# When lists are scattered and rows gathered: spacing the indirect transfers at the seam between attention and the experts

## The chip, the core and the metric

The kernel runs on one core of one Trainium2 chip. A core has five engines with queues of their own: PE (TensorE, matrix products), DVE (VectorE), ACT (ScalarE), POOL (GpSimd) and SP (SyncE, which here only issues transfers). Each engine executes its instructions strictly in the order in which they stand in its queue, and waits at an instruction until the semaphores it names have been reached. Transfers between the chip's main memory and the core's buffers are carried out by 16 DMA engines, which all queues share. Ordinary transfers are issued by SP; indirect ones, whose rows are picked by a list of indices, are issued by POOL.

The metric is the device time of one execution in microseconds (us): 654.73 us before the change, the median of three runs. One more execution was recorded by the profiler; all views of the trace come from it.

## The reference, cut to what matters

```python
# attention: B, H, S, D = 4, 8, 768, 48
f = 1.0 / (1.0 + np.exp(-f_logit))
for t in range(S):
    state = f[:, :, t, :, None] * state + np.einsum('bhd,bhe->bhde', k[:, :, t], v[:, :, t])
    y[:, :, t] = np.einsum('bhd,bhde->bhe', q[:, :, t], state)
x = y.transpose(0, 2, 1, 3).reshape(3072, 384)
# experts: E = 8, F = 1024
noisy = x @ w_gate + np.log1p(np.exp(x @ w_noise)) * noise
top2 = np.argpartition(-noisy, 2, axis=1)[:, :2]
# weights of the two: softmax over their noisy logits
for e in range(8):
    for k in range(2):
        mask = top2[:, k] == e
        h = np.maximum(x[mask] @ w1[e], 0.0)
        out[mask] += top2_w[mask, k, None] * (h @ w2[e])
```

Everything is float32. The experts see only their own tokens, so which rows an expert reads is known only after the router has run on the attention's output.

## The kernel before, in words

**Attention.** The sequence is cut into 24 pieces of work called chunks, n = 0 to 23: six blocks of 128 steps (c = n // 4) for each of four batches. A chunk passes through seven stages: `forget`, `summed`, `decays` (the gate and its running sum), `scaled` (transposes of q and k on PE), `scores` (a product and a mask), `output` (a product with v and one with the state) and `features` (the router's logits and the token rows, which go to `x_rows` in main memory). A software pipeline written out in the loop over `i` executes, in each turn, one stage of each of seven neighbouring chunks, for instance scores of chunk i, output of chunk i - 1 and features of chunk i - 2. Each execution of one stage advances a counter, `slot`. At the end of the attention fewer than seven stages are left in a turn.

**Router.** After four chunks the block c is complete, and `route(c)` runs beside the following stages, one small step per stage. Its result is, for each token and each of its two experts, a place in that expert's list. `put` then writes 128 entries (token row, weight, output row) into `lists` in main memory with one indirect transfer of POOL (L710). There are eight puts in a block and 48 in all. The waiting puts are in the list `puts`, and the loop takes one out at chosen stages. In the kernel before, one leaves every third stage until three blocks are routed (`n_routed >= HALF`), and after that one leaves at every stage:

```python
            if puts and (slot % 3 == 0 or n_routed >= HALF):
                puts.pop(0)()
```

**Experts.** An expert works on pairs of 128 rows (256 tokens). The first four pairs, p = 0 to 3, are one pair each of experts 0 to 3 and are taken from the lists of the first three blocks alone, so their work can begin before the attention ends. For a pair, `fetch(p)` (L815, issued by SP) reads 256 list entries into `slots`. It needs all 24 puts of the first half to have landed. `gather(p)` (L825, issued by POOL) reads the two halves of 128 token rows by these slots into `xg`. `turned(p, s)` (L861 and L862) transposes one half on PE and copies it into `xt_a`. `first_layer` (L913) multiplies by w1 in four groups called hp, `second_layer` (L1020) by w2 in seven products, and two indirect transfers of POOL (L1029) add the result to the output. For a later pair the transposes lie inside the second layer of the item before it. The remaining pairs, p = 4 to 23, and a few blocks of 32 rows (names ending in `_q`) follow when all 48 puts are done.

**What sets the order.** Every instruction of an engine is held in the order in which the program text emits it (`in_order`). The order is therefore written by hand: by the loop over stages, by `first_loads`, a generator that is advanced once per stage and emits the first fetches, gathers and transposes, and after the attention by the loop over `pieces`, which calls `ahead("fetch", ...)` and `ahead("gather", ...)` before each piece. As soon as `first_loads` has emitted both transposes of pair 0 (`done["turned"]`), the loop also emits the first pieces of expert 0 between the attention's last stages. Transfers are counted on eight semaphores for each kind of issuing engine, in turn: a transfer waits until the eighth before it has landed.

Weights of the first two experts are loaded in quarters by `part_of_weights` (L840, L843) during the last chunks; later ones by `weights` (L833, L835) as soon as the buffer is free.

Of the kernel before, what the change touches and what calls it, by code (L numbers as in the profile page):

```python
# [10 lines left out]
F32 = mybir.dt.float32  # L11
# [320 lines left out]
def kernel(  # L332
# [40 lines left out]
    N, DM = out.shape  # L373
# [10 lines left out]
    HALF = NCH // 2  # L384
    NP = 3 * E
    NI = 2 * E
    NE = 4
    WIDE = 4
    late_experts = (*range(NE - 1, NE - 3, -1), *range(NE, NE + WIDE), *range(NE - 3, -1, -1))
    items = [(e, [(e, 0)]) for e in range(NE)]  # L390
    items += [(e, [(e, 256 * i) for i in range(0 if e >= NE else 1, 3)]) for e in late_experts]
    pairs = [p for _, ps in items for p in ps]
    first_of = [sum(len(ps) for _, ps in items[:k]) for k in range(len(items) + 1)]
# [15 lines left out]
    moved = ctx.enter_context(tc.tile_pool(name="moved", bufs=2))  # L409
# [11 lines left out]
    def one_bank(name):  # L421
        turns.append(turns.pop(0))
        return turns[-1].tile([128, 512], F32, tag="one", name=name)
# [92 lines left out]
    xw, puts, n_put = [], [], []  # L516
# [14 lines left out]
    def clamp(n, engine=nc.gpsimd):  # L531
        if n < NCH * B:
            raw = pads["f"][n % RING["f"]][:, :, 0:D]
            engine.tensor_scalar(raw, raw, XMIN, None, ALU.max)
# [245 lines left out]
    slots, xg, xt, hcol = {}, {}, {}, {}  # L780
# [29 lines left out]
    def fetch(p):  # L810

        assert len(n_put) >= (HALF if p < NE else NCH) * B * 2
        slots[p] = ffn.tile([128, 2, 4], U32, tag=f"slots{p < NE}", name=f"slots{p}", bufs=8)
        row = pairs[p][0] * N + pairs[p][1]
        got = nc.sync.dma_start(out=slots[p], in_=lists[row:row + 256, :].rearrange("(s p) w -> p s w", p=128))  # L815
        if p < NE:

            tc.declare_no_dep(got.ins, group="later", reason="slots differ")
            tc.add_to_no_dep_group("full", got.ins)

    def gather(p):

        xg[p] = moved.tile([128, 2, DM], F32, tag="xg", name=f"xg{p}", bufs=4)
        for s in range(2):
            nc.gpsimd.indirect_dma_start(out=xg[p][:, s, :], out_offset=None, in_=x_rows[0:HALF * B * C] if p < NE else x_rows,  # L825
                                         in_offset=bass.IndirectOffsetOnAxis(ap=slots[p][:, s, 0:1], axis=0))

    def weights(k, which):
        e = items[k][0]
        if NE <= k < NE + NR:  # L830
            return
        if which == 1:
            nc.sync.dma_start(out=w1[home(k)], in_=moe_w1[e].rearrange("(k p) f -> p k f", p=128))  # L833
        else:
            nc.sync.dma_start(out=w2[home(k)], in_=moe_w2[e].rearrange("(f p) d -> p f d", p=128))  # L835
# [9 lines left out]
    def columns(k):  # L845
        side = side_of(k)
        return [[divmod(q * 256 + s * 128, side) for s in range(2)] for q in range(len(items[k][1]))]

    def item_of(p):
        return max(k for k in range(len(items)) if first_of[k] <= p)  # L850

    def turned(p, s):
        k = item_of(p)
        if k < NE:
            to = xt_a[:, :, k % 2 * 256 + s * 128:k % 2 * 256 + (s + 1) * 128]
        else:
            side, at = columns(k)[p - first_of[k]][s]
            to = (wide[0] if side else xt_a)[:, :, at:at + 128]
        xp = one_bank(f"xgp{p}_{s}")
        for i in range(KO):  # L860
            nc.tensor.transpose(xp[:, i * 128:(i + 1) * 128], xg[p][:, s, i * 128:(i + 1) * 128], ident)  # L861
        (nc.vector.tensor_copy if p < NE else nc.scalar.copy)(to, xp[:, 0:DM].rearrange("d (k t) -> d k t", k=KO))  # L862

    done = {"fetch": 0, "gather": 0, 1: NR, 2: NR, "turned": False}

    def ahead(what, until):
        if what in (1, 2):
            most = len(items) if what == 1 else done[1]
        else:
            most = min(NP if len(n_put) == NCH * B * 2 else NE, NP if what == "fetch" else done["fetch"])  # L870
        while done[what] < min(until, most):
            t = done[what]
            done[what] += 1
            fetch(t) if what == "fetch" else gather(t) if what == "gather" else weights(t, what)
# [359 lines left out]
    first = len(nc.cur_bb.bb.instructions)  # L1234
# [23 lines left out]
    def first_loads():  # L1258
        while n_routed < HALF or len(n_put) < HALF * B * 2:
            yield  # L1260
        for what, until in (("", 10), ("fetch", 1), ("", 1), ("fetch", 2), ("fetch", 3), ("", 1), ("gather", 1), ("gather", 2),
                            ("fetch", 4), ("gather", 3), ("fetch", 5), ("", 11), ("turned", 0)):
            if what == "turned":
                turned(0, 0)
                yield
                turned(0, 1)
                yield
                done["turned"] = True
            elif what:
                ahead(what, until)  # L1270
            for _ in range(1 if what else until):
                yield

    router, first_pairs = iter(()), iter(())
# [1 line left out]
    slot = n_routed = n_first = 0  # L1276
    pieces = chain.from_iterable(((k, i) for i, _ in enumerate(first_layer(k) if k < NE else first_of_two(k))) for k in range(len(items)))
    for i in range(-3, NS + 2):
        for stage, lag in ((forget, -3), (scaled, -1), (scores, 0), (summed, -2), (output, 1), (decays, -2), (features, 2)):
            n = i - lag  # L1280
            if not 0 <= n < NS:
                continue
            stage(n)
            if stage is forget:
                load("f", n + 4)
                clamp(n + 2, nc.gpsimd if n else nc.vector)
            elif stage is scaled:
                for nm in "qk":
                    load(nm, n + 2) if n < 4 else load(nm, n + 3)
                    if n == 3:  # L1290
                        load(nm, n + 3)
                if n < 2:
                    load_router(n)
                while xw:
                    xw.pop(0)()
            elif stage is scores:
                for m in (n + 1,) if n < 4 else (2 * n - 3, 2 * n - 2) if n < 6 else (n + 3,):
                    load("v", m)
                if n in (2, 6, 7, 8, 9, 10):
                    load_router(2 + (2, 6, 7, 8, 9, 10).index(n))  # L1300
                elif n == 5:
                    nc.sync.dma_start(out=lists.rearrange("(p r) w -> p r w", p=128), in_=empty)
            elif stage is output:
                if 5 <= n < 5 + NS // 2:
                    zeros(1)
            for when, first_n, whose, layer in ((scores, 17, 0, 1), (output, 18, 0, 2), (features, 20, 1, 1)):
                if stage is when and first_n <= n < first_n + 4:
                    part_of_weights(whose, layer, n - first_n)
            next(router, None)
            slot += 1  # L1310
            if puts and (slot % 3 == 0 or n_routed >= HALF):
                puts.pop(0)()
            next(first_pairs, None)

            if done["turned"] and (n_first < 5 or i >= NS - 3 and stage is not forget) and (n_first < 11 or i >= NS - 1):
                next(pieces)
                n_first += 1
        if i < 0:
            warm_up(4)
        if i >= NS - 1:  # L1320
            while xw:
                xw.pop(0)()
        n = i - 2
        if n >= 0 and n % B == B - 1:
            c = n // B
            router = chain(router, route(c))
            n_routed = c + 1
            if c == HALF - 1:
                router = chain(router, enough())
                first_pairs = first_loads()  # L1330
            if c == NCH - 1:
                router = chain(router, plan(), beyond())
# [18 lines left out]
    for item, piece in pieces:  # L1351
        p = first_of[item] + max(0, piece - 8) // 7 if item >= NE else item
        if len(zeroed) < NS and item:
            zeros(1)
        ahead("fetch", p + 6)
        ahead("gather", p + 3 if item < NE - 1 else first_of[min(item + 2, len(items))])
        n = item - NE - 2
        if 0 <= n < NQ:
            if piece == 0:
                quarter = quarter_block(n)  # L1360
            if piece % 2:
                next(quarter, None)
        if 0 <= n + 1 < NQ and piece in (9, 11, 13, 15):
            (fetch_quarter, gather_quarter, lambda n: weights_quarter(n, 1), lambda n: weights_quarter(n, 2))[(piece - 9) // 2](n + 1)
        for _ in range(1 if 3 <= piece < 7 else 2):
            next(router, None)
            if puts:
                puts.pop(0)()
# [41 lines left out]
```

## Time and profile before

| | |
|---|---|
| timed runs | 653.69, 654.73, 655.15 us |
| the profiled execution | 671.63 us, of which its span is 669.8 us |
| PE busy | 642.5 us (96%) |
| DVE, ACT, POOL busy | 442.5, 254.3, 267.5 us |
| moved by DMA | 96.31 MB, 144 GB/s on average |
| list scatters (L710) | 48, 1081 ns each on POOL |
| gathers (L825) | 48, 1124 ns each on POOL |
| output scatters (L1029) | 48, 1688 ns each on POOL |

The page of the profile gives each engine's busy time, 40 equal slices of the span (16.7 us each) in tenths, and the chain of work that ended last. A digit 9 means busy for 90% or more. The row PEclk is the clock granted to TensorE. The time of a group is the sum over its instructions; "idle before" is what the engine waited just before them, with the engine or the transfer that ended the wait. A fp32 product appears as two records of PE. Ends of products are modelled, so a busy PE is not proof of a PE at its peak. Where the engines stand in order of time, a row gives start and length in us, the engine, the line, the operation and its tiles; SPq is the issue of a transfer on SP.

The attention takes the first 180 us of the span, at about 6 us a chunk, and the experts the rest. The profiled execution is 16.9 us longer than the median of the timed runs.

### The profile page before, as it was taken

What the parts mean: (1) busy time and instruction counts of PE and PEld (TensorE: products, weight loads), DVE (VectorE), ACT (ScalarE), POOL (GpSimd) and SP (SyncE); (2) the same over time, 40 slices, a digit from 0 to 9 for tenths busy, and PEclk for the clock granted to TensorE, in tenths of its full rate; (3) what the DMA queues carried; (4) which work ended last, traced back from release to release, by engine and by line L of the source; (5) the groups of instructions that cost most, each with busy time, mean ns of one, the idle gap of its engine ahead of it and who ended that gap; (6) DMA issues with size and microseconds to landing.
All of it is one profiled execution on the core that took longest, in us unless ns stands there. A gap on an engine that the chain in (4) does not pass through costs nothing.

```text
span 669.8 us, 12902 instructions
## 1 busy us (share of the span) xinstructions
PE 642.5 (96%) x4883; PEld 553.5 (83%) x4883; DVE 442.5 (66%) x993; ACT 254.3 (38%) x603; POOL 267.5 (40%) x300
## 2 busy tenths in 40 slices
PE   8999999995999999999999999999999999999991
PEld 8999988874899998999857975896599579989891
DVE  7777858763366657777666765757576666767751
ACT  5876767641312124333333233223322332232320
POOL 7633886753056544251431441235033214512121
PEclk9999999996999999999999999999999999999997
DMA  9999988893299633364743761646093437602122
GB/s 183 187 221 205 201 172 172 170 276 90 99 345 174 151 72 70 107 176 155 240 131 114 211 166 37 247 89 187 3 309 64 122 94 222 173 15 25 22 25 29
DMA packets 153897, 96.31 MB, mean 144 GB/s; under 512 B 115600, under 2 KB 146320, under 8 KB 153824
## 3 DMA queue, kind: packets, MB, share of 16 engines
q1 hardware_dynamic: 141648, 76.12, 42.4%
q0 software_dynamic: 12176, 19.25, 14.6%
q8 instruction: 41, 0.67, 0.4%
q14 instruction: 32, 0.26, 0.1%
HBM read 75.97 MB, written 19.62 MB: 143 GB/s over the span
## 4 chain that ended last, share of the span: by engine, by line
PE 94%; DMA 2%; issue 1%; another core or an unknown queue 1%; DVE 1%; POOL 0%; SPq 0%; ACT 0%; POOLq 0%; DVEq 0%
PE y L1020 31%; PE P L938 8%; PE hp L913 7%; PE Z L938 5%; PE V L938 5%; PE X L938 5%; PE W L938 5%; PE sc L580 4%; PE xp L633 4%; PE y L598 4%; PE xgp L861 2%; PE y L609 2%; PE qp L540 2%; PE fp L540 2%; PE kp L540 2%; PE ds L604 1%
## 5 line engine op out<-in xcount | busy, mean ns | idle before, releaser
L1029 POOL DMA_INDIRECT out_dram<-ys,slots x48 | 81.0, 1688 | 181.7 <-ACT ys L1087 154.3
L1020 PE MATMUL y<-qk_all,f_all 128*128 128x192 f32 x576 | 105.2, 327 | 0.0
L1020 PEld LDWEIGHTS y<-qk_all,f_all 128*128 128x128 f32 x576 | 93.2, 190 | 0.3 <-DVE f_all L1002 0.3
L825 POOL DMA_INDIRECT xg<-x_rows,slots x48 | 53.9, 1124 | 28.2 <-issue 11.3
L1020 PE MATMUL y<-w,hs_b 128*128 128x192 f32 x320 | 59.0, 328 | 0.0
L710 POOL DMA_INDIRECT lists<-entry,sloti x48 | 51.9, 1081 | 9.9 <-issue 8.9
L1020 PEld LDWEIGHTS y<-w,hs_b 128*128 128x128 f32 x320 | 52.9, 190 | 0.9
L913 PE MATMUL hp<-xt_a,w 128*128 128x256 f32 x192 | 46.3, 398 | 6.7 <-DVE xt_a L862 6.7
L1161 POOL DMA_INDIRECT out_dram<-ys_q,slots_q x5 | 8.6, 1717 | 104.3 <-DVE ys_q L1159 104.3
L913 PEld LDWEIGHTS hp<-xt_a,w 128*128 128x128 f32 x192 | 37.5, 199 | 12.3 <-DVE xt_a L862 6.9
L974 ACT ACTIVATE hs_b<-hs_b 128x256 f32<-128x256 f32 (+1 forms) x32 | 15.1, 470 | 71.7 <-DVE hs_b L954 68.4
L938 PE MATMUL Z<-xt_b,v_all 128*128 128x256 f32 (+1 forms) x128 | 39.7, 432 | 0.0
L938 PE MATMUL X<-xt_a,w 128*128 128x256 f32 (+1 forms) x128 | 39.7, 432 | 0.0
L1079 DVE TENSOR_TENSOR ys<-P,y 128x192 f32<-128x192 f32 x24 | 8.5, 355 | 45.5 <-PE y L1020 31.1
L1087 ACT ACTIVATE ys<-ys,slots 128x384 f32<-128x384 f32 x24 | 14.8, 615 | 60.4 <-DVE ys L1086 60.4
L583 DVE TENSOR_TENSOR A<-sc,causal 128x1024 f32<-128x1024 f32 x24 | 29.3, 1222 | 11.4 <-PE sc L580 7.8
L954 DVE TENSOR_TENSOR hs_b<-hs_a,X 128x256 f32<-128x256 f32 (+1 forms) x32 | 15.6, 487 | 29.9 <-PE X L938 28.9
L1020 PE MATMUL y<-w,f_all 128*128 128x192 f32 x192 | 35.1, 326 | 0.0
L938 PEld LDWEIGHTS Z<-xt_b,v_all 128*128 128x128 f32 x128 | 24.3, 190 | 10.1
L938 PEld LDWEIGHTS X<-xt_a,w 128*128 128x128 f32 x128 | 24.3, 190 | 10.1
L954 DVE TENSOR_TENSOR hs_a<-hs_a,P 128x256 f32<-128x256 f32 (+1 forms) x64 | 31.1, 485 | 1.5
L1020 PEld LDWEIGHTS y<-w,f_all 128*128 128x128 f32 x192 | 31.9, 190 | 0.0
(199 smaller groups left out, 1443.2 us busy)
## 6 DMA issues: line engine op xcount, KB each, us to landing
w<-in_moe_w_dram SPq DMA_DIRECT2D x16, 1536.0 KB
w_q<-in_moe_w_dram SPq DMA_DIRECT2D x10, 1536.0 KB
w<-in_moe_w_dram SPq DMA_DIRECT2D x16, 384.0 KB
f_all<-in_f_logit_dram SPq DMA_DIRECT2D x24, 192.0 KB
qk_all<-in_q_dram SPq DMA_DIRECT2D x24, 192.0 KB
qk_all<-in_k_dram SPq DMA_DIRECT2D x24, 192.0 KB
v_all<-in_v_dram SPq DMA_DIRECT2D x24, 192.0 KB
x_rows<-xs SPq DMA_DIRECT2D x24, 192.0 KB
```

The costliest lines, as they stand in the source:

```text
L540: nc.tensor.transpose(p[:, cols(hp)], flat[:, cols(hp)], ident)
L580: nc.tensor.matmul(sc[:, par, cols(hp)], lhsT=kQ[n][rows(par), cols(hp)], rhs=qP[n][rows(par), cols(hp)], start=True, stop=True)
L583: nc.vector.tensor_tensor(A[n].rearrange("j r (a i) -> j (r a) i", i=C), sc.rearrange("j r (a i) -> j (r a) i", i=C), causal.unsqueeze(1). ...
L598: nc.tensor.matmul(at(hp, par), lhsT=vt[:, 2 * hp + par, :], rhs=A[n][:, par, cols(hp)], start=(hp < 2), stop=(c == 0 and hp >= HP - 2))
L633: nc.tensor.matmul(xp[:, hp, :], lhsT=yT[n][:, hp % 2, cols(hp // 2)], rhs=w_rt[:, hp, :], start=True, stop=True)
L710: into = nc.gpsimd.indirect_dma_start(out=lists, out_offset=bass.IndirectOffsetOnAxis(ap=sloti[:, r, b:b + 1], axis=0), in_=entry[:, c, b, ...
L825: nc.gpsimd.indirect_dma_start(out=xg[p][:, s, :], out_offset=None, in_=x_rows[0:HALF * B * C] if p < NE else x_rows, in_offset=bass.Indir ...
L913: nc.tensor.matmul(hp[:, o, :], lhsT=w1[home(k)][:, i, (fo + o) * 128:(fo + o + 1) * 128], rhs=xt_a[:, i, k % 2 * 256:(k % 2 + 1) * 256], ...
L938: nc.tensor.matmul(to, lhsT=x, rhs=y, start=start, stop=stop)
L954: nc.vector.tensor_tensor(to, x, y, ALU.add)
L1020: nc.tensor.matmul(P[name], lhsT=x[:, o, :], rhs=y[:, o, :], start=(o == 0), stop=(o == FH - 1))
L1029: into = nc.gpsimd.indirect_dma_start(out=out, out_offset=bass.IndirectOffsetOnAxis(ap=slots[p][:, s, 2:3], axis=0), in_=ys[s], in_offset= ...
```

## The change

Four things are different.

- A put leaves `puts` at every third stage throughout the attention. Only the blocks' order is kept; after the attention nothing changes in how they are taken out.
- `gather` can emit one half of a pair. `first_loads` is a new sequence: three stages after the last put of the first half it fetches pair 0 alone; after five stages it gathers pair 0's first half, three later the second; it fetches pair 1; four stages later come the transposes of pair 0, and then the gathers of pair 1 by halves and the fetch of pair 2. Before, the pairs 0, 1 and 2 were fetched and gathered close together and pair 3 fetched too.
- Pairs 2 and 3 are therefore gathered, and pair 3 fetched, after the attention.
- In the loop over pieces a gather is emitted only before every second piece, and only one pair at a time.

```diff
-    def gather(p):
-
-        xg[p] = moved.tile([128, 2, DM], F32, tag="xg", name=f"xg{p}", bufs=4)
-        for s in range(2):
+    def gather(p, halves=(0, 1)):
+
+        if 0 in halves:
+            xg[p] = moved.tile([128, 2, DM], F32, tag="xg", name=f"xg{p}", bufs=4)
+        for s in halves:
             nc.gpsimd.indirect_dma_start(out=xg[p][:, s, :], out_offset=None, in_=x_rows[0:HALF * B * C] if p < NE else x_rows,
...
     def first_loads():
         while n_routed < HALF or len(n_put) < HALF * B * 2:
             yield
-        for what, until in (("", 10), ("fetch", 1), ("", 1), ("fetch", 2), ("fetch", 3), ("", 1), ("gather", 1), ("gather", 2),
-                            ("fetch", 4), ("gather", 3), ("fetch", 5), ("", 11), ("turned", 0)):
-            if what == "turned":
-                turned(0, 0)
-                yield
-                turned(0, 1)
-                yield
+        for _ in range(3):
+            yield
+        for what, p, pause in (("fetch", 1, 5), ("first", 0, 3), ("second", 0, 1), ("fetch", 2, 4), ("turned", 0, 0),
+                               ("first", 1, 3), ("second", 1, 1), ("fetch", 3, 1)):
+            if what == "fetch":
+                ahead(what, p)
+            elif what == "first":
+                gather(p, (0,))
+            elif what == "second":
+                gather(p, (1,))
+                done["gather"] = p + 1
+            else:
+                for half in range(2):
+                    turned(p, half)
+                    yield
                 done["turned"] = True
-            elif what:
-                ahead(what, until)
-            for _ in range(1 if what else until):
+            for _ in range(pause):
                 yield
...
-            if puts and (slot % 3 == 0 or n_routed >= HALF):
+            if puts and slot % 3 == 0:
                 puts.pop(0)()
...
         ahead("fetch", p + 6)
-        ahead("gather", p + 3 if item < NE - 1 else first_of[min(item + 2, len(items))])
+        if piece % 2 == 0:
+            ahead("gather", min(done["gather"] + 1, p + 3 if item < NE - 1 else first_of[min(item + 2, len(items))]))
```

## The prediction

> **What bounds the kernel now.** I read the page's slices first, then the windows of 20 us, the chain of waits around the weak place, and the instructions of POOL, SP and PE there in order of time.
>
> ```profile
> PE   8999999995999999999999999999999999999991
> ...
> PEclk9999999996999999999999999999999999999997
> DMA  9999988893299633364743761646093437602122
> ```
>
> PE is full everywhere but in the tenth slice and at the two ends. The windows give the size. Columns: stretch, its length, busy time (and instructions) of PE, PEld, DVE, ACT, POOL, granted TensorE clock, DMA share, GB/s.
>
> ```profile
> 80.00:100.00 20.00, 18.60 (x267) 16.50 (x265) 13.02 (x27) 12.27 (x35) 17.92 (x27) 1.00 0.87 184
> 100.00:120.00 20.00, 19.80 (x272) 17.70 (x273) 15.62 (x37) 14.24 (x38) 14.19 (x22) 1.00 0.85 176
> 120.00:140.00 20.00, 19.06 (x273) 16.77 (x273) 17.01 (x45) 14.09 (x39) 10.95 (x19) 1.00 0.81 174
> 140.00:160.00 20.00, 11.72 (x135) 9.13 (x132) 6.17 (x10) 3.53 (x12) 15.16 (x23) 0.90 0.77 234
> 160.00:180.00 20.00, 19.00 (x132) 15.67 (x133) 7.97 (x27) 4.78 (x11) 0.00 (x0) 0.85 0.06 22
> ```
>
> From 180 to 640 us PE is busy 20.00 of every 20.00. So only 80 to 180 us, the last third of attention and its seam with the experts, can give anything back, and any PE wait put there is paid in full. The chain of waits at the seam (start, us, what):
>
> ```profile
> 139.36 1.09 PE sc L580 x16
> ...
> 153.94 1.46 PE sc L580 x2
> ...
> 155.43 0.56 DVE xt_a L862
> 155.98 3.69 another core or an unknown queue
> ...
> 161.00 5.38 PE hp L913 x12
> ```
>
> The first expert's first matmuls (hp, 12 records) cost 5.38 us instead of the 2.59 that the same group takes at 210.79 in the chain, because the clock is at half. How much is lost in all: between 140.45 (the scores of chunk 21 end) and 178.68 (the last hp group of expert 0 ends) PE executes four output groups (L598 and L609, 1.02 + 0.60 in the chain where nothing waits), three xp of 1.07, qp and kp of 0.44, two sc of 1.09, two xgp of 0.40, four hp of 2.60: 4 x 1.62 + 3 x 1.07 + 0.88 + 2.18 + 0.80 + 10.40 = 23.95 us of work in 38.23 us, so 14.3 us lost. Before it, 80 to 140 us lose 1.40 + 0.20 + 0.94 = 2.54 us.
>
> Now the clocks on the wall. The profiled execution took 671.63 us (span 669.8, and 1.83 around it); the median of the timed runs is 654.73. 671.63 - 14.3 - 2.5 = 654.8. The timed runs are as short as if PE lost nothing at the seam or before it. I conclude that these losses belong to the profiled execution and that the timed kernel already runs at PE's own pace. That is an inference from one subtraction, and the main thing that can be wrong here.
>
> [...] PE stands from 154.33 to 161.00 and the granted clock is 0.50 from 156 to 166. [...] fetch of slots issued 134.91, last packet 137.04, the gather that waits for it begins 138.53, so 1.5 us after the last byte. [...]
>
> **The change, part by part.** The built order of each engine's instructions is compared. The same instructions are executed; POOL's 48 list scatters (L710, 1.08 us each), 48 gathers (L825, 1.12 us) and SP's 24 fetches only move. PE's work is the same.
>
> 1. *Scatters every third stage.* Sixteen of the first half's 24 are spread out. POOL's sum is unchanged, PE waits for POOL there only where an output needs the state of L626, which now stands behind fewer scatters: gain in the profiled execution up to the 2.54 us, in the timed one 0, since nothing is lost. The price is lateness: in the order, scatter 24 now stands right behind the state of chunk 18, and the first fetch of slots waits for it.
>
> 2. *The chain to the first expert's rows.* Here is the new wait. The lines that price it:
>
> ```profile
> 125.48 1.26 POOL L710 DMA_INDIRECT lists<-entry,sloti  x1 [0.21 <-issue]
> ...
> 132.32 0.76 POOL L625 TENSOR_TENSOR mid<-dss,st 128x256 f32<-128x256 f32 x1 [2.94 <-ACT dss L618]
> ...
> 138.53 1.06 POOL L825 DMA_INDIRECT xg<-x_rows,slots  x1 [4.75 <-DMA v_all<-in_v_dram]
> 139.90 0.98 POOL L825 DMA_INDIRECT xg<-x_rows,slots  x1 [0.30 <-issue]
> ```
> ```profile
> 134.91 0.84 SPq L815 DMA_DIRECT2D slots<-lists  x1
> ```
> ```profile
> 149.79 0.55 PE L861 MATMUL xgp<-ident,xg 128*128 128x128 f32 x3
> ```
>
> Before: last scatter 125.48, fetch 134.91, gathers 138.53 and 139.90, their packets (records of the software queue in the trace) 141.07 to 142.66 and 143.03 to about 145.3, PE needs them at 149.79 (146.7 at its own pace): covered by more than 2 us. After, with PE's times as they stand in this profile up to 139.36:
> - State of chunk 18: 132.32 + 0.76, then L626 to 133.78. Scatter 24 starts at 133.9. From issue to last packet the scatters of the first half took 2.6 to 5.3 us by their packets, when spaced (scatters 1 to 8) 3.0 to 4.6: 136.9 to 138.5. [...] SP fetches at 137.9 to 140.0. SP would otherwise be there at about 137 (138.55 for x_rows 17 in before, less three fetches of 0.5 us). Behind it on SP wait a v load, two parts of weights and an x_rows store, none due for 5 us.
> - Slots: 3.6 us from issue to the gather in before; the next three needed 3.2 to their last packet and so 4.7. Gather, first half: 141.5 to 144.7. POOL's state of chunk 19 (done about 139.8) is not later.
> - Gather: 4.1 us to its last packet[...]. Usable at 146.0 to 150.1. PE's place for it is behind the scores of chunk 22: 140.45 + 1.62 + 1.07 + 0.88 + 1.09 = 145.11. **Wait 0.9 to 5.0 us.**
> - Second half: one scatter stands between the two gathers (1.06 + 0.3 + 1.05 + 0.6 = 3.0 us later), while PE has 0.4 + 1.62 = 2.0 us of work between the two transposes: **1.0 us more.**
>
> Sum 1.9 to 6.0 us. I take 2.8, near the lower end, because the gathers of pairs 1 and 2 (four of 0.2 MB) and three fetches no longer crowd 138 to 150 us, where the DMA share was about 1.0. Everything queued behind PE's transposes waits with it; nothing gives it back later, since PE is full to 640 us.
>
> 3. *First expert one stage earlier in PE's order.* Its hp groups now start behind features of chunk 20, not behind scores of chunk 23. Same 10.4 us; chunk 23's scores and outputs have more between them. 0 gained where nothing was lost. With it the load of the third expert's w1 (L834 in the new file, 1.5 MB) stands ahead of the x_rows stores of chunks 20 and 21 on SP. ACT's xs of chunk 23 needs the buffer of chunk 20's store: about 6.8 us of PE work after that load is released, against 1.5 MB at 340 GB/s (window 180 to 200) = 4.6 us plus the store. 0 to 1 us on ACT, hidden: its next urgent copy, P17 of expert 0, stands before it.
>
> 4. *Pairs 1 to 3 later.* Pair 1 is gathered by halves some 6 us after pair 0 and used 15 us later; pairs 2 and 3 lie between expert 0's two output scatters. They are used 20 us and more after. 0; without that cover each would cost the 5.4 us of a gather. Pair 4 now stands behind one scatter of pair 2; it waited until 234.69 for its slots anyway and the next expert has 10 us before it. 0.
>
> 5. *Every second piece, one pair at a time.* From the gather of pair 5 on, the order on POOL is identical, and POOL is in order, so 0.
>
> Sum: +2.8 us. Against the timed median 654.73 + 2.8 = **657.5 us**. Against the profiled 671.63 the same sum is 674.4 if the profiled execution loses its 16.8 us again; I expect it to lose less there.
>
> **Rivals.**
> A. The forecast: 2.0 to 4.5 us at the two transposes, 656.5 to 659.5. For it: the row of latencies above. Chance 0.5.
> B. The chain is quicker than in the loaded profile[...] and the wait is hidden: 654.7, up to 656.0. For it: the lightest DMA load. Against: SP's fetch can't start before scatter 24 has landed. Chance 0.22.
> C. Faster: the bursts of scatters do cost the timed runs. PE's losses in 92 to 126 us stand beside scatters back to back on POOL (95.28 to 99.19, 117.68 to 125.48). If they are real, spreading them returns the 2.54 us: 652.2, and part of the seam's loss could come too, down to 650. It decides when PE's losses are in the timed runs as well, which the subtraction speaks against. Chance 0.18.
> D. [...] the clock halves, as in this profile for 10 us: 3.5 + 5 = 8.5 us, 663. [...] Chance 0.1.
>
> **How the numbers follow.** About 0.2% (1.3 us) is what a measurement of this kernel can tell from no change. Slower: A and D, 0.6. Within: B, 0.22. Faster: C, 0.18. The time is A's, 657.5. Its own range is 655.8 to 660. The range for 8 in 10 leaves out most of D and the lower part of C: 651.8 to 660.8.
>
> **What would show it.** Right: in the changed profile PE waits at the transposes of the first pair (xgp), released by the gather's DMA, 1 us or more, and the fetch of the first slots on SP is released by a list scatter at 138 us or later. The windows 80 to 140 fuller on PE, with the timed median not lower, would show that the losses there are the profiler's. Wrong: xgp without a wait, and a median under 653.4 (then C) or at 654.7 (then B).

## The result, and the profile after

The changed kernel takes **660.42 us** (median of 8 runs, 657.05 to 661.6); the kernel before took 654.40 beside it (8 runs, 653.69 to 655.94). The ratio is 1.0081, 95% interval 1.0061 to 1.0101: slower, by 5.3 us from the ratio and 6.0 from the medians. The profiled execution took 658.33 us (span 656.6). Executions more than 1.5% above the fastest of their kernel are left out of all ratios (one of after_again and two of pieces below), and the profiled execution of before was one of this kind.

The slices of the page of after, over the whole span:

```profile
PE   7999999979999999999999999999999999999991
...
PEclk9999999999999999999999999999999999999996
DMA  9999988982998423368707560925275246601122
```

Apart from the two ends one weak slice of PE is left, the ninth (131 to 148 us). The windows of 20 us (columns as in the prediction) give its size:

```profile
80.00:100.00 20.00, 20.00 (x296) 18.25 (x296) 15.21 (x38) 15.14 (x41) 18.54 (x26) 1.00 0.90 201
100.00:120.00 20.00, 20.00 (x310) 18.24 (x306) 14.81 (x30) 13.32 (x36) 18.39 (x25) 1.00 0.86 191
120.00:140.00 20.00, 20.00 (x280) 17.81 (x272) 17.79 (x47) 13.50 (x38) 12.59 (x19) 1.00 0.80 189
140.00:160.00 20.00, 15.65 (x130) 12.76 (x131) 8.18 (x18) 3.06 (x8) 10.29 (x18) 0.91 0.56 150
160.00:180.00 20.00, 20.00 (x148) 18.72 (x147) 8.89 (x32) 5.28 (x12) 2.62 (x2) 1.00 0.76 252
```

PE is full from 80 to 140 us and again from 160 us. What is missing is 4.35 us of idle time and a granted clock of 0.91. PE's waits name the place (us in total, times, longest), and the chain of waits shows how it came about (start, us, what):

```profile
PE xgp L862 <- DMA xg<-x_rows,slots: 4.4, 1, 4.4
```
```profile
127.35 0.71 POOL mid L625
...
128.13 0.68 POOL st L626
...
128.97 6.08 DMA lists<-entry,sloti
...
135.06 1.73 DMA slots<-lists
...
137.61 6.70 DMA xg<-x_rows,slots
...
144.35 0.79 PE xgp L862 x3
145.13 1.91 PE y L598 x16
147.04 1.04 PE y L609 x16
148.08 0.48 PE xgp L862 x3
```

Read from the top, POOL first updates the state of a chunk and then issues scatter 24 of the lists, and 6.08 us pass until SP may fetch the slots. From the fetch to the start of the gather it takes 2.55 us (135.06 to 137.61), and from there 6.70 us until PE may transpose the gathered rows. PE stood ready at 139.99. The output group behind the transpose then takes 1.91 + 1.04 us, where the chain of before had 1.02 + 0.60. Windows of 2 us show why (last columns: granted clock, DMA share, GB/s):

```profile
142.00:144.00 2.00, 0.00 (x0) 0.00 (x0) 0.00 (x0) 0.00 (x0) 1.62 (x4) 1.00 1.00 291
144.00:146.00 2.00, 1.65 (x13) 1.32 (x15) 0.56 (x1) 0.00 (x0) 1.03 (x2) 0.63 1.05 387
146.00:148.00 2.00, 2.00 (x26) 1.37 (x22) 0.00 (x0) 0.00 (x0) 1.33 (x2) 0.52 0.94 308
```

The clock is at half just when PE resumes, from 144.52 to 147.93 in the trace's record of the clock. 3.41 us at half speed cost 1.7 us, which is also what the slow groups add up to (0.39 + 0.89 + 0.44). The wait and the half clock make 4.35 + 1.7 = 6.05 us, about the difference of the medians (6.02). That the two agree so closely is partly luck, since this one execution lies only 3.9 us above the median of before. It started early: its first scores began at 12.76 us, those of the other profiles below between 12.74 and 14.27 us. An early start is worth up to 1.5 us; where the rest of the difference comes from is not shown.

### The profile page after: what moved, and what is told of

Read it like the earlier page. It is cut to its first block, busy times and chain, and to the rows that moved or that the text cites. A ratio compares the mean times of both kernels' runs of the same rounds, so it can differ in the third digit from the quotient of the medians.

```text
span 656.6 us, 12905 instructions
## 1 busy us (share of the span) xinstructions
PE 635.6 (97%) x4883; PEld 549.1 (84%) x4883; DVE 442.6 (67%) x993; ACT 254.0 (39%) x603; POOL 272.6 (42%) x300
## 4 chain that ended last, share of the span: by engine, by line
PE 92%; DMA 4%; DVE 1%; POOL 1%; issue 1%; SPq 0%; POOLq 0%; DVEq 0%
PE y L1021 32%; PE P L939 8%; PE hp L914 6%; PE W L939 5%; PE Z L939 5%; PE V L939 5%; PE X L939 5%; PE y L598 4%; PE xp L633 3%; PE sc L580 3%; PE xgp L862 2%; PE y L609 2%; PE fp L540 1%; PE kp L540 1%; PE ds L604 1%; PE kp L574 1%
## 5 line engine op out<-in xcount | busy, mean ns | idle before, releaser
L710 POOL DMA_INDIRECT lists<-entry,sloti x48 | 55.4, 1153 | 10.6 <-issue 9.3
L914 PE MATMUL hp<-xt_a,w 128*128 128x256 f32 x192 | 43.7, 382 | 0.0
L914 PEld LDWEIGHTS hp<-xt_a,w 128*128 128x128 f32 x192 | 35.8, 190 | 4.8 <-issue 0.2
```

The source lines that it names most:

```text
L710: into = nc.gpsimd.indirect_dma_start(out=lists, out_offset=bass.IndirectOffsetOnAxis(ap=sloti[:, r, b:b + 1], axis=0), in_=entry[:, c, b, ...
L914: nc.tensor.matmul(hp[:, o, :], lhsT=w1[home(k)][:, i, (fo + o) * 128:(fo + o + 1) * 128], rhs=xt_a[:, i, k % 2 * 256:(k % 2 + 1) * 256], ...
```

## The experiments

All kernels compute the whole reference. The ratio is to runs of before on the same chip, and it is not simply the quotient of the two medians, which in sets as wide as these can lie elsewhere. On the chips of the experiments before itself spread from 654.4 to 663.5 us, in three sets of 27, 57 and 53 runs; 13, 33 and 30 of them took 659 us or more. Its first 8 runs had shown nothing of this. Stages are counted as in the loop over attention, one step of `slot` each. From the fetch of the first slots to the first transpose there are 21 in before and 13 in after, for the fetch moved seven stages later and the transposes one earlier.

The theory (T) is that this chain, with its time shortened from both ends, is all of the loss. The rivals are that spacing the scatters costs, that the moved weight load or the earlier transposes cost, and that the gathers between the pieces cost.

### Scatters early again, all else where after has it (early24)

```
-            if puts and slot % 3 == 0:
+            if puts and (slot % 3 == 0 or n_routed >= HALF and len(n_put) < HALF * B * 2):
...
-        while n_routed < HALF or len(n_put) < HALF * B * 2:
+        while slot < 144:
```

> After, but the first half's scatters 9 to 24 go one every stage, as in before; the fetch, the gathers and the transposes of the first expert stay at the stages that they have in after, so PE's and SP's orders are exactly after's. Theory T (the wait is the chain scatter 24, fetch, gather, and scatter 24's lateness starts it): SP fetches the slots at about 129.6 instead of 135.06, the gather then starts when POOL has done chunk 19's state, about 135.0 instead of 137.61, rows are usable at 140.5 to 141.7 and PE, which is there at 139.99, waits 0.4 to 1.7 us instead of 4.35, with no half clock behind: 654.4 to 656.3 us. Rival R2 (the fetches in late stages, the gathers one pair at a time or the moved weight load cost the time): the time stays at after's 660.4. Rival C (bursts of scatters cost PE time): slower than the kernel with the later transposes by 1 to 2.5 us.

Measured: 665.84 us against 658.8, ratio 1.0102 (1.0047 to 1.0157), and a wait of 10.2 us at the transpose. Putting the scatters back, alone, gives nothing back. SP's instructions in this kernel, in order of time:

```profile
133.06 1.36 SPq L528 DMA_DIRECT2D qk_all<-in_k_dram  x1
134.82 1.31 SPq L639 DMA_DIRECT2D x_rows<-xs  x1
136.19 0.43 SPq L528 DMA_DIRECT2D v_all<-in_v_dram  x1
136.66 0.72 SPq L841 DMA_DIRECT2D w<-in_moe_w_dram  x1
137.43 0.49 SPq L844 DMA_DIRECT2D w<-in_moe_w_dram  x1
138.01 0.41 SPq L639 DMA_DIRECT2D x_rows<-xs  x1
138.52 0.38 SPq L815 DMA_DIRECT2D slots<-lists  x1
```

and those of after:

```profile
129.12 0.41 SPq L639 DMA_DIRECT2D x_rows<-xs  x1
135.06 0.37 SPq L815 DMA_DIRECT2D slots<-lists  x1
```

In after's profile SP stood ready at 129.53 and waited 5.5 us for scatter 24. In early24 scatter 24 started at 126.02, and SP came to the fetch only at 138.52, by its own order: from 123.69 on it has no gap above 0.4 us, and single loads and stores take up to 2.8 us each on it (what of that is a full queue and what a wait for the data to be stored, the lines don't tell apart). SP's order is the same in both kernels. The same v load, two parts of weights and x_rows store stand ahead of the fetch; the v load is issued at 126.21 in after and at 136.19 here, while PE is only 2.4 us later (last scores before the transposes at 141.27 against 138.84).

So the fetch has two gates, the landing of scatter 24 and SP's turn, and my 129.6 took SP's free time in one profile for granted. Which gate opens last changes from execution to execution. In after_again (below) SP waited 2.2 us for the scatter. In turned_p1 (next), which keeps after's scatters, the fetch follows the store ahead of it at once, though scatter 24 had started at 129.59:

```profile
137.59 0.41 SPq L639 DMA_DIRECT2D x_rows<-xs  x1
138.10 1.44 SPq L815 DMA_DIRECT2D slots<-lists  x1
```

No run moves SP's turn alone, with the scatters left where after has them. With this, T in its first form, in which scatter 24 alone starts the chain, has failed; the theory called T2 below first puts SP's queue in its place and then the distance in stages alone.

### The transposes one stage later (turned_p1) and seven later (turned_p7)

The diff of turned_p1; turned_p7 has 11 instead of 5.

```
-("fetch", 2, 4), ("turned", 0, 0),
+("fetch", 2, 5), ("turned", 0, 0),
```

> After, with the two transposes of the first expert (and the pieces behind them) one stage later: PE comes to them behind the output group of chunk 21, which is 1.62 us of work, where before has them too. T: PE is there at 141.6 and waits 2.7 us instead of 4.35[...]: 654.4 + 2.7 = 657.1 us, 656.5 to 658. R2: 660.4. If only the length of the wait counted and the half clock stayed: 658.8.

> After, with the transposes seven stages later, scatters spaced as in after. T: no wait for the gather at all, no half clock: 654.4 us, 653.8 to 655. R1 (spacing the scatters, a scatter every third stage into the gathers' time, costs in itself): 657 or more. C (the bursts cost before something, spacing them is a gain): 652 to 653.5. R2: 658 or more.

Measured: turned_p1 664.57, ratio 1.0088 (1.0058 to 1.0118), with a wait of 8.1 us; turned_p7 659.45, ratio **0.9999** (0.9964 to 1.0034), with 0.4 us of wait in its profile. Seven stages put the time back to that of before, with the scatters spaced and everything else as in after. So spacing the scatters neither costs nor gains anything within that interval, 0.35% or 2.3 us. The run moves the transposes too, so it doesn't yet separate the distance from the early transposes; far does, below. One stage doesn't help: the waits in the profiles of this batch were about twice that of after's first profile (8.1 and 10.2 us against 4.4), so my absolute 657.1 missed.

### PE kept busy while it waits (filled)

```
         xp = one_bank(f"xgp{p}_{s}")
+        for _ in range(28 if p == s == 0 else 0):
+            nc.tensor.matmul(xp[:, 384:512], lhsT=ones, rhs=ones, start=True, stop=True)
```

> After, with 28 matmuls of ones on ones (128x128, into columns of the same bank that nobody reads) ahead of the first transpose of the first expert; nothing left out. They keep PE busy for some 3.6 to 4.2 of the 4.35 us that it waits[...], and the rows come as late as in after. T with the half clock as a part of its own: the wait stays, the 1.7 us that the transposes and output groups behind it lose at half clock go: 658.7 us, 658.2 to 659.4. If the half clock costs nothing on the path (something behind it is late anyway): 660.4. If the matmuls themselves run past the gather: 661 or more.

Measured: 667.02, ratio 1.0107 (1.0045 to 1.0168). PE in order of time, with the idle time before an instruction in brackets:

```profile
140.78 6.52 PE L862 MATMUL xgp<-ones 128*128 128x128 f32 x56
150.85 0.90 PE L864 MATMUL xgp<-ident,xg 128*128 128x128 f32 x3 [3.55 <-DMA xg<-x_rows,slots]
```

The matmuls took 6.52 us, not the 3.6 to 4.2 that I had estimated, and the rows came later still: 3.55 us of idle time were left, and the clock was at half from 149.66 to 156.49 all the same. The time is no better than that of the other kernels with 13 stages. This run doesn't separate the share of the half clock, which rests on the durations in the profiles.

### After again, and the distance made long (after_again, far)

far has the early scatters of early24 without its fixed start (`while slot < 144` is not there), so fetch and gathers go some 14 stages earlier, and the pause before `turned` is 18 instead of 4: the transposes stay at after's stage.

> After itself, unchanged, beside the same runs of before as the next three, since the chip of the last four kernels gave before 655 to 663 us. If the chip counts only through its DMA (theory T2: the first expert's rows come late because SP, in order, reaches the fetch of the slots late, its loads and x_rows stores each taking 1 to 4 us to issue while DMA is full): ratio to before 1.006 to 1.012, wait at the first transpose 4 to 11 us in the profile. If the ratio of the first runs was a matter of that chip: 1.000 or above 1.015.

> After, with scatters 9 to 24 one every stage as in before, so that the fetch and both gathers of the first expert can go some 14 stages earlier, and the transposes left at the stage that they have in after: PE's order is after's, instruction by instruction; SP's differs only in four fetches of slots, the first one ten places earlier. T2 and T (distance between scatter 24 and the transposes decides): no wait at the transposes, time of before, ratio 0.997 to 1.001. If the early transposes, the moved weight loads or the gathers by pieces cost the time: ratio 1.006 to 1.01 as after.

Measured: after_again 665.54, ratio 1.0098 (1.0069 to 1.0126), wait 5.4 us: the loss is there beside another set of runs of before. far **654.54**, ratio **0.9934** (0.9912 to 0.9957). PE's order is after's, with its earlier transposes and its hp groups between the last attention stages, and SP's has the third expert's w1 load where after has it; only the scatters, fetches and gathers are early. The early scatters alone gave nothing (early24), so it is the distance that takes the loss away. The kernel is faster than before. So neither the earlier transposes, nor the moved weight load, nor the later pairs cost anything that shows. Its profile is of the slowest of its 22 executions (659.87 us). PE doesn't wait at the transposes there, but for loads of k and q (2.3 and 1.7 us), so late transfers can cost at another place too:

```profile
PE kp L540 <- DMA qk_all<-in_k_dram: 2.3, 2, 1.2
```

### The fetch on another queue (act_fetch)

early24, and in `fetch`:

```
-        got = nc.sync.dma_start(out=slots[p], in_=lists[row:row + 256, :].rearrange("(s p) w -> p s w", p=128))
+        got = (nc.sync if p else nc.scalar).dma_start(out=slots[p], in_=lists[row:row + 256, :].rearrange("(s p) w -> p s w", p=128))
```

> The kernel with scatters 9 to 24 early and the fetch where after has it, with one thing more: the first pair's slots are fetched on ACT's DMA queue instead of SP's. T2 (SP's queue makes the fetch late): ACT issues it at about 131 to 134 instead of SP at 138.5, the gather starts 5 to 6 us earlier, the wait of 10.2 us at the first transpose falls to 3 to 5 us, ratio to before 1.003 to 1.007 instead of 1.010. Rival T3 (not the queue but the full DMA engines make each step long, so an earlier issue lands no earlier): the wait stays at 8 us or more, ratio 1.009 or more. If ACT is held up by the wait for scatter 24: PE waits for ACT instead, 1.008 or more.

Measured: 665.16, ratio 1.0108 (1.0061 to 1.0155). The wait at the transpose fell from 10.2 to 5.8 us (one profile each), but the loss stayed, and ACT, in order, was held up in its turn:

```profile
134.61 0.20 ACT L549 COPY cap<-f 128x4 f32<-128x4 f32 x1
138.06 0.42 ACTq L815 DMA_DIRECT2D slots<-lists  x1
138.52 0.65 ACT L613 COPY yT<-y 128x256 f32<-128x256 f32 x2 [3.70 <-PE sc L580]
```

ACT was free at 134.81 and issued the fetch at 138.06; what it waited for I can't read safely, since scatter 24 had started at 126.70. The DMA share was 1.02 in 135 to 140 us, as T3 would have it, but the run doesn't separate the queue from the full engines. The fetch went out only 0.5 us earlier than in early24 (138.06 against 138.52), so the run says little about SP's queue as a cause.

### The pieces alone (pieces)

before with the last hunk of the change only (`if piece % 2 == 0:` and one pair at a time).

> Before, with the last part of the change alone: in the expert phase gathers go out in every second piece, one pair at a time. Every theory but R3: no change, ratio 0.998 to 1.002, since POOL's order differs only in where gathers stand between pieces and their rows are used 20 us and more later. R3 (the gathers by pieces cost): 1.003 or more.

Measured: 656.5 against 659.81, ratio 0.9987 (0.9959 to 1.0014). No change. Its profile (an execution of 656.09 us) has before's scatters, and PE is busy for all but 0.15 us from 80 to 140 us.

### What makes the long distance better than before (before_far, first_only, far20, far_p4)

before_far is before with its fetches and gathers six stages earlier:

```
-        for what, until in (("", 10), ("fetch", 1), ("", 1), ("fetch", 2), ("fetch", 3), ("", 1), ("gather", 1), ("gather", 2),
-                            ("fetch", 4), ("gather", 3), ("fetch", 5), ("", 11), ("turned", 0)):
+        for what, until in (("", 4), ("fetch", 1), ("", 1), ("fetch", 2), ("fetch", 3), ("", 1), ("gather", 1), ("gather", 2),
+                            ("fetch", 4), ("gather", 3), ("fetch", 5), ("", 17), ("turned", 0)):
```

first_only is before with the first pair alone gathered ahead of the transposes, at before's distance:

```
+        for what, until in (("", 10), ("fetch", 1), ("", 4), ("gather", 1), ("", 11), ("fetch", 2), ("", 3),
+                            ("turned", 0), ("gather", 2)):
```

far20 is far with ten stages instead of three ahead of the fetch and a pause of 11 ahead of `turned`; far_p4 is far with a pause of 22 there.

> Before, with the fetches and gathers of its first pairs six stages earlier and the transposes where they were: PE's order is before's, the distance from the fetch of the first slots to the transposes grows from 21 stages to 27. Theory T2 (this distance alone decides; so far 13 or 14 stages gave 1.009 to 1.011, 20 gave 1.000, 27 gave 0.993): ratio 0.992 to 0.996. Rival T5 (the 27-stage kernel is faster than before because only the first pair is gathered there and the other gathers don't crowd it): 0.998 to 1.002.

> Before, with the gathers of the second and third pair (and their fetches) taken out of the time before the transposes and put behind them: PE's order and the distance of 21 stages are before's. T2: 0.998 to 1.002. T5 (the crowd of gathers makes the first one late): 0.992 to 0.996.

> The 27-stage kernel with the fetch and the gather of the first pair seven stages later, so that 20 stages lie between fetch and transposes: PE's order is still after's. T2: between the 13 stages (1.010) and the 27 (0.993), near before with its 21: 0.997 to 1.003. If only the early scatters count, or the early transposes are what makes the 27-stage kernel fast: 0.992 to 0.996 as that.

> The 27-stage kernel with the transposes four stages later, 31 stages. T2 with the wait already gone at 27: no further gain, ratio 0.992 to 0.995 and a narrower scatter of the times; if some runs at 27 stages (657 to 660 us) still waited for the gather: 0.990 to 0.993. If late transposes cost (expert 0's matmuls leave the attention stages): above 0.996.

| kernel | stages, fetch to transposes | us | ratio to before (interval) |
|---|---|---|---|
| early24 | 13 | 665.84 | 1.0102 (1.0047 to 1.0157) |
| far20 | 20 | 661.02 | 1.0039 (1.0015 to 1.0062) |
| far | 27 | 654.54 | 0.9934 (0.9912 to 0.9957) |
| far_p4 | 31 | **653.81** | **0.9916** (0.9883 to 0.9949) |
| first_only | 21 | 660.66 | 1.0009 (0.9984 to 1.0034) |
| before_far | 27 | 662.32 | 1.0057 (1.0030 to 1.0085) |

The first four have the same scatters, and the ratio falls as the distance grows. The intervals of 20 and 27 stages lie apart; those of 13 and 20 and those of 27 and 31 overlap, so that these two steps are not resolved by themselves. far_p4's runs lie between 653.52 and 655.56, beside 654.44 to 663.51 of before. All of PE's waits in its profile are at the start of the kernel:

```profile
PE warm L1243 <- DVE ones L443: 1.1, 1, 1.1
PE fp L540 <- DVE f_all L534: 0.7, 1, 0.7
```

and its windows at the seam are full:

```profile
120.00:140.00 20.00, 20.00 (x293) 17.80 (x290) 18.57 (x46) 11.77 (x33) 13.48 (x18) 1.00 0.88 195
140.00:160.00 20.00, 20.00 (x207) 17.33 (x206) 11.54 (x37) 6.66 (x19) 11.79 (x20) 1.00 1.05 279
160.00:180.00 20.00, 20.00 (x113) 18.80 (x112) 13.37 (x42) 5.24 (x12) 7.30 (x8) 1.00 0.91 289
```

first_only shows that the crowd of other gathers isn't what before suffers from. Its profile, of its slowest execution (665.33 us), also shows that before's distance of 21 stages can be too short:

```profile
PE xgp L861 <- DMA xg<-x_rows,slots: 4.4, 1, 4.4
```

before_far is the miss: the distance is 27 and the wait for the gather only 0.8 us, yet it is slower. PE's waits and the order of POOL and ACT say why:

```profile
PE xp L633 <- ACT xs L638: 5.2, 1, 5.2
...
PE xgp L861 <- DMA xg<-x_rows,slots: 0.8, 1, 0.8
```
```profile
137.66 1.96 POOL L825 DMA_INDIRECT xg<-x_rows,slots  x1 [8.11 <-DMA slots<-lists]
...
144.99 0.96 POOL L825 DMA_INDIRECT xg<-x_rows,slots  x1 [0.30 <-issue]
145.96 0.73 POOL L625 TENSOR_TENSOR mid<-dss,st 128x256 f32<-128x256 f32 x1
146.78 0.62 POOL L626 TENSOR_TENSOR st<-mid,P 128x256 f32<-128x256 f32 x1
```
```profile
147.43 0.63 ACT L559 ACTIVATE P<-L 128x512 f32<-128x512 f32 x1 [8.79 <-POOL st L626]
```

The first of six gathers waits 8.11 us on POOL for its slots, the other five follow, and the state of the chunk stands behind all six and is done at 147.40. ACT waits 8.79 us for that state, and PE for ACT. So distance alone doesn't decide: what is queued behind the waiting gather counts too. far and far_p4 put two gathers there, not six. That suggests that this part of the change, only the first expert's rows gathered ahead of the transposes, is worth having once the distance is long; no run changes the number of gathers alone at 27 stages, and at before's 21 it shows nothing (first_only).

## Why the prediction was right, and what it mis-sized

The forecast was +2.8 us, slower, by one wait at the first expert's transposes. That mechanism stands: the wait is there, released by the gather, and the fetch ahead of it was released by a list scatter (at 135.06, not at 138 or later). Taking the distance back takes the loss back (turned_p7, far). The size was too small by a factor of two: the measured 660.42 us lies above the 655.8 to 660 of the forecast's own case, and inside the full range only near its upper end.

- *PE-bound elsewhere (the subtraction).* Right for the pace: far_p4, whose PE never waits at the seam, takes 653.81 us. Right for 80 to 140 us too: PE is full there in after and nearly so in pieces, which has before's bursts, so the 2.54 us belonged to the one execution. Too strong was the conclusion that the timed kernel loses nothing at the seam. Over half of the runs of before in two later sets took 659 us or more, and the profiles at its distance show waits for the gather from 0.8 us (pieces) to 4.4 us (first_only). That all of before's spread comes from there is likely but not shown. The profile of 671.63 us is no example of it: its transposes did not wait for the gather, PE lost 6.67 us at the first hp behind a copy on DVE, 3.69 of them to a release that the trace doesn't name, and it took 8 us longer than the slowest timed run of before. Its clock dropped at 155.89, 1.6 us after PE had gone idle at 154.33, and stayed at half for 10.24 us.
- *Step 1, scatters.* 0, right within 0.35% (turned_p7). Rival C's gain of 2.54 us, a ratio of 0.9961, falls just outside that interval.
- *Step 2, the chain.* From scatter 24 to PE's place I had 145.11 - 133.9 = 11.2 us; after shows 139.99 - 128.97 = 11.0. The chain itself I had at 12.1 to 16.2; it took 15.4. The term that was mis-sized is the choice inside it, 2.8, "near the lower end", of which 1.8 were for this wait where 4.35 came, on the ground that the gathers of pairs 1 and 2 and three fetches leave DMA emptier. Scatter to fetch took 6.08 (I had 4.0 to 6.1) and gather to PE 6.70 (4.5 to 5.4); only fetch to gather was shorter, 2.55 (3.6 to 4.7). The ranges are estimates: of the time from a transfer's last packet to the start of what waits for it, the prediction measured the 1.5 us of the slots alone. DMA was no emptier when the gather ran: its share was 0.94 to 1.00 from 140 to 144 us, though those gathers were gone.
- *The second half, +1.0.* Not seen: at half clock PE's work between the two transposes took 2.95 us, not 1.62, and by then the second half was there.
- *Rival D, the half clock.* I gave it as 0.1 and as a case of its own, with 3.5 us of wait and 5 us of cost. It came with the forecast's wait, for 3.41 us, at a price of 1.7. A and a small D together make the 6.05. It belonged in the sum: every profile with a wait of 3.3 us or more at the first transpose has the half clock behind it (far20 3.3, after 4.4, up to early24 10.2), and those with 0.8 or less (pieces, turned_p7) have none there.
- *SP's queue.* The prediction put SP at the fetch "at about 137" if nothing held it, and then followed scatter 24 alone. Either can be the later one (the scatter in after, SP's turn in turned_p1), so moving the scatters alone gave nothing (early24).
- *Steps 3, 4 and 5.* 0, right: far has steps 3 and 4 and loses nothing by them that shows, and pieces has step 5 alone.

Two things stay open: why the transfers take longer in some executions, which decides whether a kernel with 13 stages waits 4 us or 10; and how far_p4 compares with before where before does not wait (653.81 beside 654.40 of another set is no comparison).

## What to carry to other kernels

A chain of small dependent transfers (list scatter, fetch of indices, indirect gather) took 15 to 16 us here from the last scatter to the first transpose (after, after_again). Count its distance to the consumer in stages of the compute engine, from the program place of the first issue, and leave some room: 13 stages lost about 1% here, 20 and 21 still showed waits in some profiles, and 31 showed none in its profile and the narrowest spread of times. A transfer can have two gates, the data that it needs and its engine's turn; moving one of them tells little while the other can be the later one. An in-order engine that waits for such a transfer holds up what is queued behind it (in before_far POOL waited 8.11 us for the slots, and then ACT 8.79 for the state behind the gathers), so put as little as can be behind the waiting instruction.

## What the runs showed of the hardware

The time at half clock came in whole steps in these profiles. Apart from the end of the kernel, the clock was at half for 3.41 us in after and far20, 6.83 in after_again, filled, before_far and first_only, 10.24 in before, turned_p1 and act_fetch, 13.65 in early24: one, two, three and four times 3.41. The drop came 4.5 us after PE had gone idle in after (139.99 to 144.52), 2.4 in filled, 2.3 in early24 (142.43 to 144.75), 2.2 in after_again (141.46 to 143.62) and 1.6 in before. So it has no fixed distance from the start of the idle time in these runs; what decides it is not shown, nor how short an idle time can be and still bring a drop. For a sum it follows that a wait can bring time at half clock with it (the shortest at the first transpose that did was far20's 3.3 us, while 0.8 us in pieces and 0.4 in turned_p7 did not), and that the 3.41 us that PE spent at work at half clock in after cost 1.7 us.

The step from the fetch of 4 KB of slots to the start of the gather took 2.55 us in after (135.06 to 137.61), where SP had issued nothing from 129.53 to 135.06 and the DMA share was 0.65 in 135 to 140 us; 3.45 in far_p4 (131.89 to 135.34, share 0.79 in 130 to 135); and, with shares of 0.94 to 1.02 in 135 to 140, 4.4 in after_again, 5.5 in act_fetch and 7.0 in early24. The longer steps are those with the higher shares, but not in their order, and no run here shows what lengthens them.
